# Merged last products, a kept key tile, last queries turned with their keys, and a plain product at the end: one change to an attention and two-MLP kernel

## The chip, the cores and the metric

The kernel runs on one core of a Trainium2 chip. The metric is the device time of one execution in microseconds (us); the median of three runs is compared.

## The reference

```python
# q, k, v: 4 batches x 8 heads x 576 positions x 64, fp32
scores = scale * q @ k.T                       # within a head
mask = (rel >= 0) & (rel < 128)                # a window of 128 keys, causal
scores = where(mask, scores - slope[h] * abs(rel), -1e9)
attn = softmax(scores)                         # sum + 1e-9 in the denominator
x = (attn @ v)  -> [2304 tokens, 512]
x = relu(x @ w_in) ** 2 @ w_out                # 512 -> 2048 -> 512
out = (sigmoid(x @ w_gate) * (x @ w_val)) @ w_out2   # 512 -> 1536 -> 512
```

The weights arrive as 64-bit words and are turned to fp32 in the kernel. Every product of the two MLPs is made of three products of halves (high x high, high x low, low x high).

## The kernel before, in words

**Attention.** The 576 queries of a batch are cut into kinds: "a" (queries 0 to 255), "b" (256 to 511) and "c" (the last 64). A unit is a pair of heads (HP = 4 pairs) of one kind of one batch; a "c" unit takes all four pairs at once. `turn` loads queries and keys of two pairs, transposes them on TensorE (tile `tq` for queries, `tk` for keys; for "c" both go to `tq`, with 64 and 96 rows) and copies them on ScalarE to `qs` and `ks` (`ka` for kind "a", which the "b" units of the same batch read again as their first 128 keys). `attend` then makes the scores (`ts`, lines 638 and 653), masks and adds the slopes on VectorE, takes exp on ScalarE, normalizes, transposes the probabilities (`tp`, line 741), copies them to `pt`, masks them with POOL's selection (line 751), multiplies by the values (`tv`, line 778) and splits the result into a high and a low half of `x` (one ScalarE copy, one VectorE subtraction). An fp32 product is two instructions on TensorE, and the two heads of a pair use different halves of the array's rows or columns, so their instructions stand in pairs.

**First MLP.** The tokens are cut into eight chunks: batch 0 a, batch 0 b, batch 1 a, batch 1 b, then four of 320 tokens that take a "c" part too. For each chunk, 16 steps of `h_step` (tile `h`, lines 804 to 806) and `y_step` (tile `y`, line 841). `h_step` evicts with relu, squares, and splits into `gs`. Attention of later chunks stands between the steps of earlier ones.

**Second MLP.** One block of 256 tokens (`gv`, `o_step`) and four of 512, which use Strassen's seven products: `gv_strassen` for the gate and value products (tiles `pa`, `pd`, line 962), whose result `cg` is split into `ah` with sums `ss`, and `o_strassen` for the output (tiles `o` P1 to P7, line 1120). `sums` loads the summed weights (`so`, `st`) from a scratch in memory. After the last step come two more parts of the last block for pair f = F2 - 4 (one of them) and f = F2 - 2 (both), and then the additions in `oc` and the stores.

**Order.** Nothing is executed in source order. Each operation is registered with `op(...)`: the engines it may run on with a price in ns, what it reads and writes, and a priority (`prio`, a due time in steps). `Plan.schedule` is a list scheduler: it advances a clock, starts on each engine the ready operation of least priority value, and hands out buffers from pools of slots (`CAP` and `CAP0` cap how many a kind may hold; `CAP0` is for chunks 0 to 2). Its order is the order of instructions on each engine. While nothing else is ready in the first 21 us it puts in warm-up products (`warm`). Prices that the change touches: a turn 4 x `pe_ns(128)` = 223 ns, "a" scores 12 x `pe_ns(256)` = 1309 ns, "b" scores 16 x `pe_ns(256)` = 1745 ns.

Of the kernel before, what the change touches and what calls it, by code (L numbers as in the profile page):

```python
# [287 lines left out]
def attention_moe_moe2_kernel(ctx: ExitStack, tc, q, k, v, w_in, w_out1, w_gate, w_val, w_out2, out):  # L288
    nc = tc.nc
# [26 lines left out]
    CAP = {"raw": 3, "nq": 1, "nk": 1, "qs": 2, "ks": 2, "ka": 2, "wt": 6, "vs": 3, "st": 4, "pt": 2, "t": 3,  # L316
           "h": 2, "y": 4, "pg": 2, "pv": 2, "o": 6, "pa": 1, "pd": 1, "pa2": 1, "pd2": 1, "xacc": 2, "ob": 2, "ysg": 2, "raw2": 2, "pp": 2, "xp": 2,
           "tg": 2, "tw": 2, "st2": 5, "so": 5, "xf": 6, "cg": 4, "ss": 2, "ah": 12, "oc": 4, "qc": 3}
    CAP0 = {"nq": 3, "nk": 3, "qs": 2, "ks": 2, "ka": 3, "vs": 5, "st": 5, "pt": 6, "t": 6}
# [220 lines left out]
    X, TURNED, VT = {}, {}, {}  # L540
    FINE = 0

    def values(b, kind, chunk, prio):
# [7 lines left out]
        for h0, h1 in ((0, H // 2), (H // 2, H)) if chunk < FINE else ((0, H),):  # L551
            for t, vn in tiles.items():
                m = min(128, S - 128 * t)
                op({"SP": 250 + 60 * (h1 - h0)}, lambda e, vn=vn, t=t, m=m, h0=h0, h1=h1: nc.sync.dma_start(
                    out=vn()[0:m, h0:h1], in_=v[b, h0:h1, 128 * t:128 * t + m, :].rearrange("h p d -> p h d")),
                   w=[(vn, "v", h) for h in range(h0, h1)], prio=prio, data=182 / 2 * (h1 - h0) * m / 128)

    def turn(b, kind, g, chunk, p):

        early = chunk < 3  # L560
        nq, vq, vk = (2, 128, 128) if kind != "c" else (1, S - 512, (S - 384) // 2)
        a_q, a_k = {"a": (0, 0), "b": (256, 256), "c": (512, 384)}[kind]

        turns = ((0, 1), (1, 2)) if chunk < FINE else ((0, 2),)
        loaded = []
        for src, a, nt, r, name in ((q, a_q, nq, vq, "nq"), (k, a_k, 2, vk, "nk")):
            loaded.append((new(name, [128, nt, 4, 64], F32, early), src, a, nt, r))
        for i0, i1 in turns:
            for t, src, a, nt, r in loaded:
                op({"SP": 250 + 250 * (i1 - i0)}, lambda e, t=t, src=src, a=a, nt=nt, r=r, i0=i0, i1=i1: nc.sync.dma_start(  # L570
                    out=t()[0:r, :, 2 * i0:2 * i1], in_=src[b, 4 * g + 2 * i0:4 * g + 2 * i1, a:a + r * nt, :].rearrange("h (p j) d -> p j h d", j=nt)),
                   w=[(t, i) for i in range(i0, i1)], prio=p(0) - 3, data=2.85 * nt * r * (i1 - i0))

        qs = new("qs", [128, 2, nq * vq], F32, early)
        ks = new("ka" if kind == "a" else "ks", [128, 2, 2 * vk], F32, early)
        banks = [new("tq", [128, 512], F32, early)] * 2 if kind == "c" else [new(kd, [128, 512], F32, early) for kd in ("tq", "tk")]
        parts = ((qs, nq, vq, 0), (ks, 2, vk, 2 * vq if kind == "c" else 0))

        def flip(e, which, i0, i1):
            for z in which:  # L580
                _, nt, v_, c0 = parts[z]
                for i in range(i0, i1):
                    for j in range(nt):
                        nc.tensor.transpose(banks[z]()[:, c0 + (i * nt + j) * v_:c0 + (i * nt + j + 1) * v_],  # L584
                                            loaded[z][0]()[0:v_, j, 2 * i:2 * i + 2].rearrange("p h d -> p (h d)"), C["ident"][0:v_, 0:v_])

        c0 = parts[1][3]
        for i0, i1 in turns:
            for which in ((0, 1),) if kind == "c" else ((0,), (1,)):
                op({"PE": sum(parts[z][1] * 2 * (i1 - i0) * pe_ns(parts[z][2]) for z in which)}, lambda e, which=which, i0=i0, i1=i1: flip(e, which, i0, i1),  # L590
                   cols=.5, r=[(loaded[z][0], i) for z in which for i in range(i0, i1)], w=[(banks[z], z, i) for z in which for i in range(i0, i1)],
                   prio=p(1 + which[0] / 2), also=[parts[z][0] for z in which])
            for i in range(i0, i1):
                op({"ACT": act_ns(nq * vq, True) + 94}, lambda e, i=i: nc.scalar.activation(
                    out=qs()[:, i].rearrange("c (p j) -> c j p", j=nq),
                    in_=banks[0]()[:, i * nq * vq:(i + 1) * nq * vq].rearrange("c (j p) -> c j p", j=nq), func=AF.Copy,
                    scale=C["qmul"][:, 2 * g + i:2 * g + i + 1]), r=[(banks[0], 0, i)], w=[(qs, i)], prio=p(1.3))
            op({"ACT": act_ns(2 * vk * (i1 - i0), True)}, lambda e, i0=i0, i1=i1: nc.scalar.activation(
                out=ks()[:, i0:i1].rearrange("c i (p j) -> c i j p", j=2),
                in_=banks[1]()[:, c0 + 2 * vk * i0:c0 + 2 * vk * i1].rearrange("c (i j p) -> c i j p", i=i1 - i0, j=2), func=AF.Copy),  # L600
               r=[(banks[1], 1, i) for i in range(i0, i1)], w=[(ks, i) for i in range(i0, i1)], prio=p(1.8))
        TURNED[b, kind, g] = qs, ks

    def attend(u, due, long):
# [14 lines left out]
        vkeys = [(t_, "v", h) for t_ in vt.values() for hp in u.hps for h in (2 * hp, 2 * hp + 1)] + [(t_, "pad") for t_ in vt.values()]  # L619
# [4 lines left out]
        def plain(pr):  # L624
# [4 lines left out]
            kprev = TURNED[u.b, "a", groups[0]][1] if kind == "b" else None  # L629

            def go(e):
                if kind == "c":

                    for g, (qs, ks) in enumerate(turned):
                        for x in range(2):
                            for i in range(2):
                                rows = slice(64 * i, 64 * i + 64)
                                nc.tensor.matmul(both[g]()[rows, 256 * x:256 * x + S - 384], qs()[rows, x], ks()[rows, x], start=True, stop=True)
                    return
                qs, ks = turned[0]  # L640
                x = u.hps[0] % 2
                for j in range(nq):

                    if j > 0:
                        todo = [(ks, 0, 0, 256)]
                    elif kind == "b":
                        todo = [(kprev, 128, 0, 128), (ks, 0, 128, 128)]
                    else:
                        todo = [(ks, 0, 0, 128)]
                    for src, k0, c, w_ in todo:  # L650
                        for i in range(2):
                            rows = slice(64 * i, 64 * i + 64)
                            nc.tensor.matmul(both[i]()[:, 256 * j + c:256 * j + c + w_], qs()[rows, x, j * 128:(j + 1) * 128],  # L653
                                             src()[rows, x, k0:k0 + w_], start=True, stop=True)

            mine = sorted({hp % 2 for hp in u.hps})
            rd = [(k_, i) for t_ in turned for k_ in t_ for i in mine] + ([(kprev, i) for i in mine] if kind == "b" else [])
            op({"PE": {"a": 12 * pe_ns(256), "b": 16 * pe_ns(256), "c": 16 * pe_ns(S - 384) + 100}[kind]}, go, r=rd, w=both, prio=pr, also=[st, sm], cols=.5)
# [58 lines left out]
        N = 256  # L717
        cols = 64 if kind == "c" else 128
        if kind == "c":
            xpart = lambda z: x()[:, z, :, n0:n0 + 64]  # L720
        else:
            xpart = lambda z: x()[:, z, u.hps[0], n0:n0 + 256]
        xout = lambda z: [(x, z, hp, u.part) for hp in u.hps]
# [32 lines left out]
        for j in range(nq):  # L756
            if u.q0 + j > 0:
                sel(j, "prev")
            sel(j, "own")
        vp = new("tv", [128, 512], F32, early)  # L760


        prods = []
        if kind != "c":
            h0 = 2 * u.hps[0]
            prods.append((u.q0, h0, lambda i: mid()[:, i].rearrange("p j c -> p (j c)"), 0, 256, True, False))
            if u.q0 > 0:
                prods.append((u.q0 - 1, h0, lambda i: ends()[:, i, 0], 0, 128, False, False))
            prods.append((u.q0 + 1, h0, lambda i: ends()[:, i, 1], 128, 256, False, True))
        else:  # L770
            for hp in u.hps:
                prods.append((3, 2 * hp, lambda i, hp=hp: ends()[:, 2 * hp + i, 0], 64 * hp, 64 * hp + 64, True, False))
                prods.append((4, 2 * hp, lambda i, hp=hp: mid()[:, 2 * hp + i, 0], 64 * hp, 64 * hp + 64, False, True))

# [5 lines left out]

        op({"PE": sum(4 * pe_ns(pr_[4] - pr_[3]) + 46 for pr_ in prods) + 54}, go, cols=.5, r=vkeys + ks_,
           w=[vp], prio=p(9), also=[x])
        if kind == "c":
            vpart = lambda: vp()[:, :N].rearrange("p (c t) -> p c t", t=64)
        else:
            vpart = lambda: vp()[:, :N]
# [145 lines left out]
    def sums(n, kind, f, prio):  # L932
        after = [W["out2", F2 - 4, 22], ("scr", ("out2", F2 - 2), 7)] if n == 1 and f == 0 else []
        TW[n, kind, f] = dict(zip(("P6", "P7", "P5", "P4"),
# [9 lines left out]
    def gv_strassen(n, kind, f, e0):  # L944
# [86 lines left out]

        p3 = new("ah", [128, 512], F32R)
# [75 lines left out]
    def o_strassen(n, f, part, e0, last=False):  # L1108


        t0, NB = blocks[n]
        ops, wts = A2[n, f], TW[n, "out2", f]
# [12 lines left out]
        for i in range(6 * part, 6 * part + 6):  # L1125
            name, t = OO[i // 2], i % 2
            o = O[n][name]
            op({"PE": 3 * pe_ns(256)}, lambda e, name=name, t=t, o=o: go(name, t, o, f == 0, f == F2 - 2),
# [153 lines left out]
```

## Time and profile before

| | us |
|---|---|
| median of 3 runs | 970.33 (968.18 to 972.26) |
| the profiled execution, whole | 969.7 |
| its span, first to last instruction | 967.9 |
| TensorE busy in the span | 950.9 (98%) |
| VectorE, ScalarE, POOL busy | 622.3, 566.3, 192.0 |

The prediction is read against the profiled execution; the 1.8 us around its span belong to the time too. A matmul's duration overlaps the next one, so the distance between starts is the price of one.

### The profile page before, as it was taken

The page shows a single profiled execution, that of the slowest core. Times are in us where ns is not written, and L with a number is a line of the kernel's source. Part 1 is how long each engine was busy: PE and PEld are TensorE (multiplying, and loading weights), DVE is VectorE, ACT ScalarE, POOL GpSimd, SP SyncE. Part 2 cuts the span into 40 slices and gives each one's busy share as a digit, 9 for nine tenths or more (in the row PEclk, how much of TensorE's full clock was granted, in tenths as well). Part 3 has the DMA queues.
Part 4 walks back from the last instruction along what each step waited for, and adds up shares of the span by engine and source line. Part 5 has one row for each costly group of instructions (what it writes and reads, how often), then busy time and mean ns, then how long its engine had stood idle before and what let it go on. Part 6 is the DMA issues. An engine that isn't in the chain of part 4 may idle for free.

```text
span 967.9 us, 21379 instructions
## 1 busy us (share of the span) xinstructions
PE 950.9 (98%) x7728; PEld 913.6 (94%) x7728; DVE 622.3 (64%) x1608; ACT 566.3 (59%) x1496; POOL 192.0 (20%) x277
## 2 busy tenths in 40 slices
PE   8899999999999999999999999999999999999997
PEld 6589999989999998999999999999999999999997
DVE  7999986777676687677552133645765585476555
ACT  6988777668677677576654422544544544454442
POOL 3611112223224112112200000102211230222001
PEclk9989999999999999999999999999999999999999
DMA  9765446584664873963599941566776687678931
GB/s 229 174 178 163 151 121 206 175 264 160 193 206 158 230 213 133 264 209 136 158 348 376 385 143 34 189 215 225 252 254 210 214 279 223 212 241 264 348 113 45
DMA packets 181929, 200.64 MB, mean 207 GB/s; under 512 B 80192, under 2 KB 113472, under 8 KB 181824
## 3 DMA queue, kind: packets, MB, share of 16 engines
q1 hardware_dynamic: 181824, 199.27, 65.1%
q8 instruction: 62, 1.02, 0.4%
q14 instruction: 43, 0.35, 0.1%
HBM read 152.04 MB, written 47.19 MB: 206 GB/s over the span
## 4 chain that ended last, share of the span: by engine, by line
PE 91%; ACT 3%; DMA 2%; DVE 2%; POOL 1%; SPq 1%; issue 0%; POOLq 0%; DVEq 0%; ACTq 0%
PE y L841 21%; PE pa L962 14%; PE pd L962 11%; PE o L1120 10%; PE h L804 7%; PE h L805 7%; PE h L806 7%; PE tv L778 3%; PE ts L653 2%; PE o L1087 2%; PE pd L1120 2%; PE tp L741 1%; PE tq L584 1%; ACT st L685 1%; DMA nq<-in_q_dram 1%; DMA wscr<-pp 1%
## 5 line engine op out<-in xcount | busy, mean ns | idle before, releaser
L841 PE MATMUL y<-gs,wh 128*128 128x256 f32 (+1 forms) x1024 | 216.0, 303 | 3.7 <-DVE gs L335 2.8
L841 PEld LDWEIGHTS y<-gs,wh 128*128 128x128 f32 x1024 | 165.1, 191 | 10.3 <-issue 4.8
L804 PE MATMUL h<-x,wh 128*128 128x256 f32 (+1 forms) x512 | 155.0, 303 | 0.6 <-ACT pt L745 0.6
L841 PE MATMUL y<-gs,wl 128*128 128x256 f32 (+1 forms) x512 | 152.2, 297 | 0.0
L805 PE MATMUL h<-x,wh 128*128 128x256 f32 (+1 forms) x512 | 151.2, 295 | 0.0
L806 PE MATMUL h<-x,wl 128*128 128x256 f32 (+1 forms) x512 | 151.1, 295 | 0.0
L338 ACT ACTIVATE cg<-pa 128x256 f32<-128x256 f32 x144 | 54.8, 382 | 109.4 <-PE pa L962 105.9
L335 DVE TENSOR_TENSOR gs<-r,gs 128x320 fp32r<-128x320 f32 (+1 forms) x115 | 54.7, 475 | 72.1 <-ACT gs L338 71.6
L804 PEld LDWEIGHTS h<-x,wh 128*128 128x128 f32 x512 | 96.7, 189 | 4.2 <-issue 1.9
L841 PEld LDWEIGHTS y<-gs,wl 128*128 128x128 f32 x512 | 97.7, 191 | 0.0
L818 ACT ACTIVATE r<-h 128x256 f32<-128x256 f32 (+1 forms) x128 | 51.9, 406 | 76.8 <-PE h L806 76.3
L805 PEld LDWEIGHTS h<-x,wh 128*128 128x128 f32 x512 | 96.7, 189 | 0.0
L806 PEld LDWEIGHTS h<-x,wl 128*128 128x128 f32 x512 | 96.6, 189 | 0.0
L962 PE MATMUL pa<-x,st 128*128 128x256 f32 x576 | 84.2, 282 | 0.0
L751 POOL TENSOR_SCALAR_AFFINE_SELECT pt<-pt 128x256 f32<-128x256 f32 (+1 forms) x120 | 62.8, 549 | 106.5 <-ACT pt L745 105.5
L978 DVE TENSOR_TENSOR cg<-cg,pd 128x256 f32<-128x256 f32 x96 | 40.4, 421 | 61.0 <-PE pd L962 59.7
L962 PEld LDWEIGHTS pa<-x,st 128*128 128x128 f32 x576 | 75.1, 189 | 0.0
L1120 PE MATMUL o<-wr,ah 128*128 128x256 f32 x432 | 70.4, 281 | 0.2 <-DVE ah L335 0.2
L1120 PE MATMUL o<-so,ah 128*128 128x256 f32 x432 | 66.3, 281 | 0.0
L685 ACT ACTIVATE st<-st,sm 128x128 f32<-128x128 f32 x144 | 56.4, 397 | 10.7 <-DVE sm L678 10.7
L338 ACT ACTIVATE gs<-r 128x256 fp32r<-128x256 f32 (+1 forms) x128 | 56.6, 442 | 9.1 <-PE y L841 2.6
L1120 PEld LDWEIGHTS o<-wr,ah 128*128 128x128 f32 x432 | 59.5, 189 | 0.4 <-DVE ah L335 0.4
(179 smaller groups left out, 2050.4 us busy)
## 6 DMA issues: line engine op xcount, KB each, us to landing
st<-wscr SPq DMA_DIRECT2D x192, 256.0 KB, 3.4
wscr<-pp SPq DMA_DIRECT2D x72, 512.0 KB, 3.4
so<-wscr SPq DMA_DIRECT2D x96, 256.0 KB, 3.5
raw<-in_moe_w_out_dram SPq DMA_DIRECT2D x28, 512.0 KB, 3.8
wr<-wscr SPq DMA_DIRECT2D x54, 256.0 KB, 5.4
raw<-in_moe_w_in_dram SPq DMA_DIRECT2D x16, 512.0 KB, 4.7
vs<-in_v_dram SPq DMA_DIRECT2D x24, 256.0 KB, 5.1
raw<-in_moe_w_gate_dram SPq DMA_DIRECT2D x12, 512.0 KB, 4.3
```

Of the source, the lines that this page charges most:

```text
L335: return lambda e: eng(e).tensor_tensor(out=out(), in0=a(), in1=b(), op=ALU.subtract)
L338: return lambda e: nc.scalar.activation(out=out(), in_=in_(), func=AF.Copy, scale=scale)
L685: op({"ACT": 386}, lambda e, x=x: nc.scalar.activation(out=st()[:, x, :], in_=st()[:, x, :], func=AF.Exp, bias=sm()[:, x:x + 1], scale=-1. ...
L751: op({"POOL": pool_sel(512 // nq)}, lambda e: nc.gpsimd.affine_select(out=pt_of(what, j), in_=pt_of("own", j), pattern=[[0, 512 // (nq * c ...
L804: nc.tensor.matmul(ps()[:, :N], w[0]()[:, c], x()[:, 0, cc, :N], start=cc == 0, stop=False)
L805: nc.tensor.matmul(ps()[:, :N], w[0]()[:, c], x()[:, 1, cc, :N], start=False, stop=False)
L806: nc.tensor.matmul(ps()[:, :N], w[1]()[:, c], x()[:, 0, cc, :N], start=False, stop=cc == CC - 1)
L818: op({"ACT": act_ns(N, True)}, lambda e: nc.scalar.activation(out=g()[:, :N], in_=ps()[:, :N], func=AF.Relu), r=[ps], w=[g], prio=ep, also ...
L841: nc.tensor.matmul(y()[:, c0:c0 + N], w[a]()[:, c], gs()[:, b, :N], start=f == 0 and p == 0 and n != 1, stop=f == F1 - 1 and p == 2, skip_ ...
L962: nc.tensor.matmul(ps()[:, :256], w()[:, z * 256 + cc * 128:z * 256 + cc * 128 + 128], x, start=start and cc == 0 and i == 0, stop=cc == 1 ...
L978: op({"DVE": dve_ns(256)} if psum else dve_or_pool(256), lambda e: eng(e).tensor_tensor(out=quarter(i, j)(), in0=quarter(i, j)(), in1=src( ...
L1120: nc.tensor.matmul(o()[:, 256 * t:256 * t + 256], a_()[:, c_ + 128 * t:c_ + 128 * t + 128], w()[:, 256 * z:256 * z + 256], start=start and ...
```

## The change

There are four edits and new prices for the scheduler. (1) From chunk 3 on, the last product of an even unit ("a" or "b") is put off until the odd unit of its two pairs is ready; both go into one bank `tv` in one operation, and one copy and one subtraction of 512 columns move them to `x`. (2) The "b" turn writes its keys into two tiles of 384 columns, one for each pair; a copy on ScalarE or POOL puts the last 128 keys of the "a" tile ahead of them. The "b" scores then read one tile: two products of 256 columns for each head instead of one of 256 and two of 128. (3) For "c", one tile holds the 64 last queries and the 64 last keys, another the 128 keys before; four transposes of 128 rows a turn replace six, and both tiles are loaded once for a batch. (4) For the last pair of the last block, the seven Strassen products are replaced by eight plain ones; the sums of the earlier pairs' products are taken in `oc` before it, the results added as they come, and the last one stored in two halves. Prices: a turn 436, scores of "a" and "b" 1056, of "c" 1643 ns. `pt` may hold 4 slots instead of 2, `ks` 3 instead of 2.

```diff
-    CAP = {..."ks": 2, ... "pt": 2, ...}
+    CAP = {..."ks": 3, ... "pt": 4, ...}
-    CAP0 = {... "ks": 2, ...}
+    CAP0 = {... "ks": 4, ...}
...
+    MERGE = 3
...
     def turn(b, kind, g, chunk, p):
...
+            qs = new("qs", [128, 2, 256], F32, early)
+            ks = [new("ka", [128, 2, 256], F32, early)] if kind == "a" else [new("ks", [128, 384], F32, early) for _ in range(2)]
...
+                op({"PE": 436}, flip, cols=.5, r=[loaded[z]], w=[bank], prio=p(1 + z / 2), also=[qs] if z == 0 else ks)
...
+                else:
+                    for i in range(2):
+                        op({"ACT": act_ns(256, True)}, lambda e, i=i, bank=bank: nc.scalar.activation(
+                            out=ks[i]()[:, 128:384].rearrange("c (p j) -> c j p", j=2),
+                            in_=bank()[:, 256 * i:256 * i + 256].rearrange("c (j p) -> c j p", j=2), func=AF.Copy), r=[bank], w=[(ks[i], 1)], prio=p(1.8))
...
+                def carry(e, i=i):
+                    if e == "ACT":
+                        nc.scalar.activation(out=ks[i]()[:, 0:128], in_=before[i]()[:, 128:256], func=AF.Copy)
+                    else:
+                        nc.gpsimd.tensor_copy(ks[i]()[:, 0:128], before[i]()[:, 128:256])
...
+        if g == 0:
+            own, prev = LAST[b] = new("nq", [128, H, 64], F32, early), new("nk", [128, H, 64], F32, early)
+            for t, src, r0, a0, n in ((own, q, 0, 512, S - 512), (own, k, S - 512, 512, S - 512), (prev, k, 0, 384, 128)):
...
+        def flip(e):
+            for z, t in enumerate((own, prev)):
+                for i in range(2):
+                    nc.tensor.transpose(bank()[:, 256 * z + 128 * i:256 * z + 128 * i + 128],
+                                        t()[:, 4 * g + 2 * i:4 * g + 2 * i + 2].rearrange("p h d -> p (h d)"), C["ident"])
...
+                    k0, w_ = (128 * j, 256) if kind == "b" else (0, 128 + 128 * j)
+                    for i in range(2):
+                        rows = slice(64 * i, 64 * i + 64)
+                        nc.tensor.matmul(both[i]()[:, 256 * j:256 * j + w_], qs()[rows, x, j * 128:(j + 1) * 128],
+                                         ks[x]()[rows, k0:k0 + w_], start=True, stop=True)
...
-            op({"PE": {"a": 12 * pe_ns(256), "b": 16 * pe_ns(256), "c": 16 * pe_ns(S - 384) + 100}[kind]}, go, r=rd, w=both, prio=pr, also=[st, sm], cols=.5)
+            op({"PE": {"a": 1056, "b": 1056, "c": 1643}[kind]}, go, r=rd, w=both, prio=pr, also=[st, sm], cols=.5)
...
+        PROBS[u.b, kind, u.hps[0]] = mid, ends
+        both = kind != "c" and u.chunk >= MERGE
+        if both and u.hps[0] % 2 == 0:
+            return
         vp = new("tv", [128, 512], F32, early)
...
+        hps = [u.hps[0] - 1, u.hps[0]] if both else u.hps
...
     def sums(n, kind, f, prio):
+        if (n, kind, f) == (nblk - 1, "out2", F2 - 2):
+            TW[n, kind, f] = {ij: W[kind, f, ij] for ij in (11, 21, 22)}
+            TW[n, kind, f][12] = fetch("so", (kind, f), PIECE[kind][12], prio, after)
+            return
...
+        if (n, f) == (nblk - 1, F2 - 2):
+            A2[n, f] = {}
+            for i in (1, 0):
+                hi, lo = new("ah", [128, 512], F32R), new("ah", [128, 512], F32R)
+                for j in range(2):
+                    cs = slice(256 * j, 256 * j + 256)
+                    op({"ACT": act_ns(256)}, copy(lambda hi=hi, cs=cs: hi()[:, cs], quarter(i, j)), r=[(c[i], j)], w=[(hi, j)], prio=pr, also=[lo])
+                    op({"DVE": dve_ns(256)}, minus(lambda lo=lo, cs=cs: lo()[:, cs], quarter(i, j), lambda hi=hi, cs=cs: hi()[:, cs]),
...
+        if n == nblk - 1 and f == F2 - 4 and part == 1:
+            u, u3, v, w = OC[n] = [new("oc", [128, 512], F32) for _ in range(4)]
+            op({"ACT": act_ns(512, True)}, copy(u, o["P1"]), r=[o["P1"]], w=[u], prio=pr)
+            add(u3, u, o["P6"])
+            add(v, u3, o["P7"])
+            add(u3, u3, o["P5"])
+            add(w, v, o["P5"])
...
+    def o_last(n, f, part, e0):
+        if part == 0:
+            todo = [(1, 0, PAD["pd"], v, True), (1, 1, PAD["pa"], w, True)]
+        else:
+            todo = [(0, 0, o["P2"], u, False), (0, 1, o["P3"], u3, False)]
+        for z, (i, j, ps, sum_, fresh) in enumerate(todo):
+            fine = (i, j) == (0, 1)
+            for t in range(2):
+                for part_ in range(2):
+                    (hi, ch, kh), (lo, cl, kl) = ops[i, part_]
+                    wt = wts[10 * part_ + 11 + j]
...
+                    op({"PE": 3 * pe_ns(256)}, go, r=[(hi, kh), (lo, kl), wt, ps], w=[ps if not fine else (ps, t)],
+                       prio=e0 + z + .2 * t + .1 * part_)
...
```

## Rows read from the trace of the kernel before

**Rows 1.** The page: its head and the busy table's first line.

```profile
span 967.9 us, 21379 instructions
...
PE 950.9 (98%) x7728; PEld 913.6 (94%) x7728; DVE 622.3 (64%) x1608; ACT 566.3 (59%) x1496; POOL 192.0 (20%) x277
```

**Rows 2.** Stretches: us, PE, PEld, DVE, ACT, POOL busy (count), clock, DMA, GB/s.

```profile
20.00:30.00 10.00, 9.60 (x90) 6.25 (x87) 8.81 (x48) 10.00 (x40) 6.28 (x10) 1.00 0.95 234
...
45.00:50.00 5.00, 2.16 (x17) 1.79 (x14) 4.82 (x18) 5.00 (x21) 1.96 (x4) 0.79 0.52 99
50.00:55.00 5.00, 5.00 (x27) 4.78 (x28) 4.77 (x13) 2.70 (x6) 0.00 (x0) 0.53 0.70 200
...
300.00:500.00 200.00, 200.00 (x1526) 186.57 (x1525) 135.89 (x388) 134.58 (x366) 40.68 (x66) 1.00 0.65 203
```

**Rows 3.** Timeline of TensorE near 48 us: start, duration, instruction, idle before.

```profile
48.67 0.58 PE L841 MATMUL y<-gs,wh 128*128 128x256 f32 x1 [2.84 <-DVE gs L335]
```

**Rows 4.** Timeline of TensorE: one burst of an "a" unit's last products.

```profile
145.90 0.28 PE L806 MATMUL h<-x,wl 128*128 128x256 f32 x1
146.11 0.87 PE L778 MATMUL tv<-pt,vs 128*64 128x256 f32 x8
146.91 0.38 PE L841 MATMUL y<-gs,wh 128*128 128x256 f32 x1
```

**Rows 5.** The same, two "a" units that stand together.

```profile
143.75 1.52 PE L778 MATMUL tv<-pt,vs 128*64 128x256 f32 x16
145.20 0.39 PE L804 MATMUL h<-x,wh 128*128 128x256 f32 x1
```

**Rows 6.** Timeline of TensorE: a "c" turn, and an "a" turn's queries.

```profile
312.62 0.31 PE L806 MATMUL h<-x,wl 128*128 128x320 f32 x1
312.86 0.33 PE L584 MATMUL tq<-identr,nq 64*128 64x64 f32 x2
313.13 0.55 PE L584 MATMUL tq<-identr,nk 96*128 96x96 f32 x4
313.46 0.54 PE L841 MATMUL y<-gs,wh 128*128 128x320 f32 x2
...
339.88 0.31 PE L806 MATMUL h<-x,wl 128*128 128x320 f32 x1
340.03 0.60 PE L584 MATMUL tq<-identr,nq 128*128 128x128 f32 x4
340.39 0.54 PE L841 MATMUL y<-gs,wh 128*128 128x320 f32 x2
```

**Rows 7.** Timeline of TensorE: the scores of a "b" unit.

```profile
419.22 0.49 PE L653 MATMUL ts<-ka,qs 64*128 64x128 f32 x4
419.55 0.82 PE L653 MATMUL ts<-ks,qs 64*128 64x128 f32 x8
420.30 0.56 PE L841 MATMUL y<-gs,wh 128*128 128x320 f32 x2
```

**Rows 8.** Groups by line and form: count, busy us, mean ns, idle before.

```profile
L598 ACT ACTIVATE ks<-tk 128x512 f32<-128x512 f32 x8 | 5.2, 646 | 1.6 <-PE tk L584 1.6
```

**Rows 9.** Timeline of POOL in the first microseconds: a copy.

```profile
3.11 0.28 POOL L397 COPY relc<-rel 64x128 f32<-64x128 f32 x1
```

**Rows 10.** Timeline of the last 12 us, all engines.

```profile
955.75 0.42 DVE L335 TENSOR_TENSOR ah<-cg,ah 128x256 fp32r<-128x256 f32 x1
955.84 1.10 PE L1120 MATMUL o<-wr,ah 128*128 128x256 f32 x8
...
957.16 1.45 PE L1120 MATMUL o<-wr,ah 128*128 128x256 f32 x10 [0.23 <-DVE ah L335]
...
960.28 3.46 DVE L1145 TENSOR_TENSOR oc<-o,oc 128x512 f32<-128x512 f32 x5
...
961.27 0.87 PE L1120 MATMUL o<-wr,ah 128*128 128x256 f32 x6
...
963.28 1.26 POOL L1169 TENSOR_TENSOR oc<-oc,xacc 128x512 f32<-128x512 f32 x1 [4.68 <-DVE oc L1145]
```

More of the change, by code (lines that the diff above doesn't have):

```diff
@@ L550, in values @@
                 op({"POOL": 150 + 2.1 * 512}, lambda e, vn=vn, m=m: nc.gpsimd.memset(vn()[m:128], 0.0), w=[(vn, "pad")], prio=prio)
-        for h0, h1 in ((0, H // 2), (H // 2, H)) if chunk < FINE else ((0, H),):
+        for h0, h1 in ((0, H),):
             for t, vn in tiles.items():
@@ L556, in values @@
                    w=[(vn, "v", h) for h in range(h0, h1)], prio=prio, data=182 / 2 * (h1 - h0) * m / 128)
+    LAST = {}
     def turn(b, kind, g, chunk, p):
         early = chunk < 3
[L561 to L601, printed above, removed]
@@ new lines, in turn @@
+        m = S - 512
+        qs, ks, bank = new("qs", [128, 2, m], F32, early), new("ks", [128, 2, 128 + m], F32, early), new("tq", [128, 512], F32, early)
+        def flip(e):
+            for z, t in enumerate((own, prev)):
+                for i in range(2):
+                    nc.tensor.transpose(bank()[:, 256 * z + 128 * i:256 * z + 128 * i + 128],
+                                        t()[:, 4 * g + 2 * i:4 * g + 2 * i + 2].rearrange("p h d -> p (h d)"), C["ident"])
+        op({"PE": 436}, flip, cols=.5, r=[(own, 0), (own, m), (prev, 0)], w=[bank], prio=p(1), also=[qs, ks])
@@ new lines, in turn @@
+        for i in range(2):
+            op({"ACT": act_ns(m, True) + 94}, lambda e, i=i: nc.scalar.activation(
+                out=qs()[:, i], in_=bank()[:, 128 * i:128 * i + m], func=AF.Copy, scale=C["qmul"][:, 2 * g + i:2 * g + i + 1]),
+               r=[bank], w=[(qs, i)], prio=p(1.3))
+        for z, (c0, c1) in enumerate(((128, 128 + m), (0, 128))):
+            op({"ACT": act_ns(2 * (c1 - c0), True)}, lambda e, z=z, c0=c0, c1=c1: nc.scalar.activation(
+                out=ks()[:, :, c0:c1], in_=bank().rearrange("c (z i p) -> c z i p", z=2, i=2)[:, z, :, (128 - m if z == 0 else 0):], func=AF.Copy),
+               r=[bank], w=[(ks, z)], prio=p(1.8))
@@ L604, in attend @@
+        TURNED[b, kind, g] = qs, [(lambda i=i: ks()[:, i]) for i in range(2)], [[(ks, 0), (ks, 1)]] * 2
     def attend(u, due, long):
@@ L628, in plain @@
             turned = [TURNED[u.b, kind, g] for g in groups]
-            kprev = TURNED[u.b, "a", groups[0]][1] if kind == "b" else None
             def go(e):
                 if kind == "c":
-                    for g, (qs, ks) in enumerate(turned):
+                    for g, (qs, ks, _) in enumerate(turned):
                         for x in range(2):
@@ L716, in attend @@
         n0 = 256 * u.part
-        N = 256
         cols = 64 if kind == "c" else 128
[L719 to L723, printed above, removed]
         shape = [128, 2, 2, 128] if kind != "c" else [128, 2 * HP, 1, 64]
@@ L1111, in o_strassen @@
         t0, NB = blocks[n]
+        if (n, f) == (nblk - 1, F2 - 2):
+            return o_last(n, f, part, e0)
+        stop_at = F2 - 4 if n == nblk - 1 else F2 - 2
         ops, wts = A2[n, f], TW[n, "out2", f]
@@ L1172, in attention_moe_moe2_kernel, with go @@
     OC = {}
+    def o_last(n, f, part, e0):
+        t0, NB = blocks[n]
+        ops, wts, o = A2[n, f], TW[n, "out2", f], O[n]
+        u, u3, v, w = OC[n]
+        if part == 0:
[8 more added lines that the diff above has]
+                    wt = wts[10 * part_ + 11 + j]
+                    def go(e, t=t, part_=part_, hi=hi, lo=lo, ch=ch, wt=wt, ps=ps, fresh=fresh):
+                        for k, (a_, y) in enumerate(((hi, 0), (hi, 1), (lo, 0))):
+                            nc.tensor.matmul(ps()[:, 256 * t:256 * t + 256], a_()[:, ch + 128 * t:ch + 128 * t + 128], wt()[:, 256 * y:256 * y + 256],
+                                             start=fresh and t == 0 and part_ == 0 and k == 0, stop=part_ == 1 and k == 2, skip_group_check=True)
+                    op({"PE": 3 * pe_ns(256)}, go, r=[(hi, kh), (lo, kl), wt, ps], w=[ps if not fine else (ps, t)],
+                       prio=e0 + z + .2 * t + .1 * part_)
+                if fine or t == 1:
+                    cs = slice(256 * t, 256 * t + 256) if fine else slice(0, 512)
+                    key = (ps, t) if fine else ps
+                    op({"DVE": dve_ns(256 if fine else 512)}, lambda e, ps=ps, sum_=sum_, cs=cs: nc.vector.tensor_tensor(
+                        out=sum_()[:, cs], in0=ps()[:, cs], in1=sum_()[:, cs], op=ALU.add), r=[key, sum_], w=[(sum_, t) if fine else sum_], prio=e0 - 2)
+                    r0, m = t0 + 256 * i + (128 * t if fine else 0), 128 if fine else 256
+                    op({"SP": 475}, lambda e, sum_=sum_, cs=cs, r0=r0, m=m, j=j: nc.sync.dma_start(
+                        out=out[r0:r0 + m, 256 * j:256 * j + 256].rearrange("(t p) c -> p t c", p=128),
+                        in_=sum_()[:, cs].rearrange("p (t c) -> p t c", c=256)), r=[(sum_, t) if fine else sum_], prio=e0, data=728)
     WA = [("in", 0)]
```

100 lines of the change are left out of this document (66 added, 34 removed).

## The prediction

> **What bounds the kernel now.** I read four things, from the whole to the single instruction.
>
> First the page's busy table: TensorE is busy 98% of a span of 967.9 us [rows 1]. A busy share alone doesn't show a bound, so second the table of stretches. From 300 to 500 us TensorE is busy all 200 us at full clock, while VectorE and ScalarE are busy 136 and 135 of 200 [rows 2]. There a copy more or less on those two costs nothing, and a TensorE slot saved is time saved. The start is different: from 20 to 30 us ScalarE is busy 10.0 of 10 us and VectorE 8.8; from 45 to 50 us TensorE works only 2.2 us and its granted clock is 0.79, then 0.53 up to 55 us, which means mostly the lower of its two levels, 1.2 instead of 2.4 GHz [rows 2]. Third, the timeline there names the cause: a y product at 48.67 us waited 2.84 us for VectorE's gs [rows 3]. Fourth, since TensorE is the bound, I need the price of each small group of products. The "busy" of a pipelined matmul overlaps its neighbour (0.28 us long, but 0.12 us after the last one), so I take prices from start to start in the timeline.
>
> **Merged last products (chunks 3 to 7: 20 units in 10 pairs).** The columns are the same; what goes is one of two bursts. A lone burst of a kind "a" unit starts 0.21 us after the last h product, where 0.12 is the spacing, and the y product follows 0.80 us later: 1.01 in all, so the burst costs 1.01 - 0.12 = 0.89 [rows 4]. Two such units that happened to stand together, 16 instructions, took 1.45 from their first to the next h product [rows 5]: the second eight add 1.45 - 0.80 = 0.65. A merge saves 0.89 - 0.65 = 0.24. Where the burst already stands behind scores, its entry (0.21 - 0.12 = 0.09) is saved anyway, so 0.15. Ten pairs: 1.5 to 2.4; I take 2.1, nearer the upper end, as most bursts stand alone. The even unit waits for the odd one; its copies to x come later, but the last unit of a chunk comes when it did, with one 512-wide copy and one subtraction in place of two each. ScalarE and VectorE have a third of their time free there [rows 2].
>
> **Last queries turned with their keys (8 turns).** Six transposes (two with 64 rows, four with 96) become four with 128. Before: 312.62 to 313.46 is 0.84, less one h slot of 0.15 (a slot of 320 columns: 339.88 to 340.03): 0.69. Four full transposes: 339.88 to 340.39 is 0.51, less 0.15: 0.36 [rows 6]. Saving 0.33 a turn, 2.7 in all; as bounds 2.4 (a slot or two at the old entry price) and 2.8. The four loads per batch become three, on SP, which isn't late there; the one copy of keys becomes two on ScalarE, covered as above.
>
> The Trainium skill speaks for and against here. "TensorEngine Tiling (Array Packing)", Key Properties, says that a change of tiling mode drains TensorE, which agrees with the 0.21 and 0.24 us entries [rows 4, 6]. "TensorE: Matmul & The Clock Gate", Back-to-back issue gap, prices a product by its columns, N/2.4 + 2.5 ns: by that, six transposes (my estimate 228 ns) and four (223 ns) cost the same and the saving is nothing. The measured 0.69 against 0.36 decides; the rule is kept as a rival.
>
> **Kept key tile (16 "b" units).** Scores were six pairs of passes, four 128 and two 256 wide; now four 256 wide. Of the 1.08 us, the two 128 pairs from the "a" tile take 0.33 and the rest, two of 128 and two of 256, 0.75 [rows 7]. With 0.09 for leaving (as for entering, rows 4) and a 256 pair twice a 128 pair, 6c = 0.66, c = 0.11: so the first two carry 0.11 over their columns. After: 8c + 0.09 = 0.97, saving 0.11. If a 256-wide first pair pays the same 0.11, nothing is saved. A 256 pair already lasts 0.22, longer than that first pair did, so I take 0.11. Only 12 of the units lie in the stretch that TensorE bounds; the four of batch 0 lie at 20 to 35 us. So 0 to 1.3, taken 1.3. The price is on the other engines: each of 8 turns evacuates keys in two ScalarE copies where one took 0.65 [rows 8], and adds two copies of 128 columns on POOL or ScalarE; the nearest row is POOL's copy of 64x128 in 0.28 [rows 9]. From 60 us on that is covered [rows 2]. In the first 45 us ScalarE has no cover: two turns, each some 0.2 us of fixed cost, and four carries of about 0.3: from nothing (they land on POOL between selections) to 1.6 us. I take 0.3.
>
> **Eight products at the end.** Seven Strassen products of 6 instructions (42) become eight of 6 (48): 6 x 0.12 = 0.7 more. Removed: four combinations and the halves that hang on them. TensorE's wait there, 0.23 us in the row and 0.4 with the lost slots [rows 10], ends with it, because the first of the new operands are plain quarters, split as soon as the gating multiply ends. So TensorE ends at about 962.14 + 0.7 - 0.4 = 962.4. Behind it, before: VectorE's row of five additions of 0.69 ends at 963.74, then POOL adds from 963.28 to 964.54, and store and closing take 967.9 - 964.54 = 3.4 [rows 1, 10]. After: half an addition, 0.42 (a 256-wide VectorE pass [rows 10]), then the same 3.4 or a little less for half the bytes: 962.4 + 0.1 + 0.4 + 3.4 = 966.3, a gain of 1.6. What can be late is VectorE: from 955.05 it has four splits of 0.42, the addition to xacc, three to four of the sums taken in advance and five final ones: 1.7 + 0.7 + 2.8 + 2.9 = 8.1 us, to about 963.1 where 962.9 is needed. So 0.7 to 2.1, taken 1.4. Three loads of weights fewer are hidden.
>
> **The start.** Everything is placed by a list scheduler whose prices change: a turn 223 to 436 ns, "a" scores 1309 to 1056, "b" scores 1745 to 1056. So the order of the first 60 us can change although the work hardly does. What lies there to win or lose is the wait of 2.8 us and the slow stretch behind it: from 48.67 to 55 us, some 6 us, at about half the clock, so some 3 us more than at the higher level [rows 2, 3]. Bounds: 6 us gained, 6 lost; I take none, and the 0.3 above.
>
> **Sum.** 2.1 + 2.7 + 1.3 + 1.4 - 0.3 = 7.2 us. The profiled execution took 969.7 us (span 967.9, 1.8 around it): 962.5. The median of the three runs shown is 0.6 above that execution, so 963.1; call it 963.0. A measurement of this kernel tells about 0.5%, 4.9 us, from no change: below 965.5 is faster, above 975.2 slower.
>
> **Rivals.**
> - *The start reorders against us.* The gs wait gets longer or the scores of batch 0 wait for carried keys, and 2.5 to 5 us are lost: 965.5 to 968. For it: ScalarE has no free time from 20 to 30 us. Against it: the added work is 1.6 us at most. Chance 0.17, a quarter of it still below 965.5.
> - *The start reorders for us.* gs comes early enough, the clock doesn't fall at 48 us, 3 to 6 us are gained: 957 to 960. Chance 0.12.
> - *TensorE goes by columns.* All three edits of the attention keep their columns (512 for a "c" turn, 512 per "b" scores, merged products likewise). If the entries are paid anyway, in other places, only the tail is left: 969.7 - 1.4 = 968.3, with the median's 0.6 about 968.9. Against it are rows 4 to 6, where neighbours are the same and the bursts differ. Chance 0.07. (The skill's rule on the issue gap says this.)
> - *Slower: a second slow stretch.* The same y wait at the start, on VectorE's gs, lasts so long that chunk 1's products also run at 1.2 GHz. One stretch like the present one costs 2.8 + 3 = about 6 us [rows 2, 3]; the gain of 7.2 is gone when that y product starts later than about 56 us instead of 48.67. One and a half such stretches more give 972, two give 975. Against it: loads and first turns don't change. Chance 0.05, half of it above 975.2.
>
> The forecast itself, 960.5 to 965.5, has 0.59.
>
> **Numbers.** Below 965.5: 0.59 + 0.12 + 0.04 = 0.75. Above 975.2: 0.02, rounded to 0.03. Between: 0.22. Range: from 958.5, which leaves half of the good start out (0.06), to 967.8, which leaves out the rivals by columns and slower and little else (0.13).
>
> **What would show it.** Right: "c" turns with four transposes and 0.36 between neighbours; ten bursts of 16 or 24 tv instructions at 0.65 to 0.85 for the second unit; "b" scores of eight instructions in about 0.97; the y product of rows 3 near 48 us; TensorE ending with its last product, one half addition and one store behind it, 3.9 us to the end. Wrong: a TensorE wait in the middle for x or a bank held by an unmerged pair, that y product several us later, or VectorE ending far behind TensorE in the tail.

## The result and the profile after

The changed kernel takes 958.49 us (median of 3 runs, 957.54 to 959.99) against 970.33: a ratio of 0.9882 [0.9856, 0.9908], so it is faster by 11.8 us where 7.3 were forecast. That is the very edge of the range ("from 958.5"), outside the forecast itself (960.5 to 965.5), and the time of the rival in which the start reorders for us. The profiled execution took 957.54, its span 955.4.

The page, as [rows 1]:

```profile
span 955.4 us, 21188 instructions
...
PE 941.8 (99%) x7656; PEld 908.9 (95%) x7656; DVE 630.4 (66%) x1621; ACT 559.8 (59%) x1496; POOL 186.4 (20%) x270
```

The stretches, as [rows 2]:

```profile
20.00:30.00 10.00, 9.13 (x78) 6.33 (x78) 8.99 (x57) 10.00 (x44) 5.54 (x13) 1.00 1.05 235
45.00:50.00 5.00, 3.90 (x34) 2.76 (x32) 4.82 (x18) 3.73 (x14) 0.01 (x1) 1.00 0.12 44
50.00:55.00 5.00, 3.94 (x33) 3.06 (x34) 4.90 (x26) 3.91 (x16) 1.93 (x2) 1.00 0.65 171
300.00:500.00 200.00, 200.00 (x1515) 189.62 (x1515) 136.79 (x378) 129.17 (x353) 38.09 (x60) 1.00 0.67 204
```

In the middle nothing has changed its kind: TensorE works all 200 us, the other engines have a third of their time free. At the start it has: from 45 to 55 us the granted clock stays at 1.00, the level of 2.4 GHz, where it was 0.79 and 0.53. The y product that waited 2.84 us at 48.67 [rows 3] starts at 41.27 after 1.28. TensorE's timeline, its waits between 41 and 55 us:

```profile
41.27 0.39 PE L870 MATMUL y<-gs,wh 128*128 128x256 f32 x1 [1.28 <-DVE gs L335]
...
50.57 0.92 PE L679 MATMUL ts<-ka,qs 64*128 64x128 f32 x6 [1.36 <-DVE x L335]
...
54.84 0.39 PE L834 MATMUL h<-x,wh 128*128 128x256 f32 x1 [0.49 <-DVE x L335]
```

**Small groups of products.** From the same timeline, a "c" turn, "b" scores, and merged last products of "a" and of "b" units, each with its neighbours:

```profile
303.48 0.31 PE L835 MATMUL h<-x,wl 128*128 128x320 f32 x1
303.63 0.38 PE L624 MATMUL tq<-identr,nq 128*128 128x128 f32 x2
...
304.42 0.54 PE L870 MATMUL y<-gs,wh 128*128 128x320 f32 x2
...
356.06 0.31 PE L870 MATMUL y<-gs,wl 128*128 128x320 f32 x1
356.30 1.52 PE L806 MATMUL tv<-pt,vs 128*64 128x256 f32 x16
357.75 0.41 PE L833 MATMUL h<-x,wh 128*128 128x320 f32 x1
...
408.92 1.13 PE L679 MATMUL ts<-ks,qs 64*128 64x256 f32 x8
409.98 0.41 PE L833 MATMUL h<-x,wh 128*128 128x320 f32 x1
...
430.98 0.31 PE L870 MATMUL y<-gs,wl 128*128 128x320 f32 x1
431.21 1.96 PE L806 MATMUL tv<-pt,vs 128*64 128x256 f32 x24
433.10 0.56 PE L870 MATMUL y<-gs,wh 128*128 128x320 f32 x2
```

Both "c" turns of a batch stand together: 304.42 - 303.48 less a slot of 0.15 is 0.79, so 0.40 a turn against 0.69 [rows 6]. Two merged "a" units cost 357.75 - 356.06 - 0.15 = 1.54, against twice 0.89 [rows 4]: 0.24 saved, as the two of [rows 5]. The "b" scores are what was misjudged: 408.92 to 409.98 is 1.06, against 1.08 [rows 7]. They save 0.02, not 0.11. The starts of the single products in the two traces show why: before, the first two instructions of 128 columns (one for each head) stand 0.21 us ahead of the next two, and those only 0.11 ahead of the ones behind them; after, the first two of 256 columns stand 0.32 ahead, the next two 0.22. The first step costs 0.10 more at either width.

**The copies.** Groups by line and form:

```profile
L338 ACT ACTIVATE x<-tv 128x512 fp32r<-128x512 f32 x10 | 5.9, 591 | 3.9 <-PE tv L806 3.8
L594 ACT ACTIVATE ks<-tk 128x256 f32<-128x256 f32 x16 | 5.7, 402 | 1.7 <-PE tk L580 1.7
L604 ACT ACTIVATE ks<-ka 128x128 f32<-128x128 f32 x13 | 3.7, 300 | 0.0
```

Ten merges, as counted. The keys of a turn take 2 x 402 ns where one copy took 646 [rows 8], so 0.16 more, and 13 of the 16 carries (the copies of the "a" tile's last keys) went to ScalarE at 0.30 each, near POOL's 0.28 [rows 9]; the three on POOL took 0.46.

**The end**, as [rows 10]: VectorE and TensorE in the timeline of the last 12 us.

The multiply before, and then the end of the changed kernel:

```profile
954.35 0.69 DVE L1007 TENSOR_TENSOR cg<-cg 128x512 f32<-128x512 f32 x1
```

```profile
943.47 0.69 DVE L1040 TENSOR_TENSOR cg<-cg 128x512 f32<-128x512 f32 x1
...
945.53 0.60 PE L1254 MATMUL pd<-wr,ah 128*128 128x256 f32 x3
...
948.44 1.58 PE L1254 MATMUL o<-wr,ah 128*128 128x256 f32 x12
...
951.12 0.42 DVE L1262 TENSOR_TENSOR oc<-o,oc 128x256 f32<-128x256 f32 x1 [0.37 <-PE o L1254]
...
951.60 0.62 PE L1254 MATMUL o<-wr,ah 128*128 128x256 f32 x3 [0.52 <-DVE oc L1262]
952.25 0.43 DVE L1262 TENSOR_TENSOR oc<-o,oc 128x256 f32<-128x256 f32 x1 [0.71 <-PE o L1254]
```

From the gating multiply (943.47; 954.35 before) TensorE needs 8.75 us to its end at 952.22, where it needed 7.79. Behind it come one half addition and a store: 3.2 us to the end of the span, where there were 5.8. There is a wait that nobody forecast: the last three products wait 0.52 us for VectorE to read the first half of the bank `o`, though they write the other half.

**Where the time went.** I cut each trace at two marks: the start of the product that follows the first 600 of the first MLP (`h` and `y`), and the first product of the second MLP. The first two stretches are called the start and the middle below.

| us | to product 600 | to the second MLP | to the end | span |
|---|---|---|---|---|
| before | 132.1 (130.9) | 416.8 (418.0) | 419.0 | 967.9 |
| after | 125.9 | 411.8 | 417.7 | 955.4 |
| gained at equal work | 5.0 | 6.2 | 1.4 | 12.5 |
| forecast | -0.3 | 6.1 | 1.4 | 7.2 |

Before had one "b" unit's scores more behind it at the first mark, 1.32 less a slot of 0.15 = 1.17 us; in brackets the times with that moved over. The last two columns came as forecast. All that was missed lies in the first 130 us.

### The profile page after: what moved, and what is told of

Its sections match the earlier page's. It is cut to its first block, busy times and chain, and to the rows that moved or that the text cites. A ratio compares the mean times of both kernels' runs of the same rounds, so it can differ in the third digit from the quotient of the medians.

```text
span 955.4 us, 21188 instructions
## 1 busy us (share of the span) xinstructions
PE 941.8 (99%) x7656; PEld 908.9 (95%) x7656; DVE 630.4 (66%) x1621; ACT 559.8 (59%) x1496; POOL 186.4 (20%) x270
## 4 chain that ended last, share of the span: by engine, by line
PE 94%; DVE 3%; ACT 1%; DMA 1%; SPq 1%; issue 0%; DVEq 0%
PE y L870 22%; PE pa L995 14%; PE pd L995 11%; PE o L1168 10%; PE h L833 7%; PE h L834 7%; PE h L835 7%; PE tv L806 3%; PE ts L679 2%; PE o L1132 2%; PE pd L1168 2%; PE tp L761 1%; DMA nq<-in_q_dram 1%; ACT st L711 1%; PE ts L670 1%; PE pv L1104 1%
## 5 line engine op out<-in xcount | busy, mean ns | idle before, releaser
L335 DVE TENSOR_TENSOR gs<-r,gs 128x256 fp32r<-128x256 f32 (+1 forms) x122 | 58.0, 476 | 64.7 <-ACT gs L338 64.4
L1168 PE MATMUL o<-wr,ah 128*128 128x256 f32 x414 | 68.0, 281 | 0.0
L1168 PE MATMUL o<-so,ah 128*128 128x256 f32 x414 | 64.0, 281 | 0.0
L1168 PEld LDWEIGHTS o<-wr,ah 128*128 128x128 f32 x414 | 57.3, 189 | 0.0
```

The lines of the kernel that those rows point to most:

```text
L335: return lambda e: eng(e).tensor_tensor(out=out(), in0=a(), in1=b(), op=ALU.subtract)
L1168: nc.tensor.matmul(o()[:, 256 * t:256 * t + 256], a_()[:, c_ + 128 * t:c_ + 128 * t + 128], w()[:, 256 * z:256 * z + 256], start=start and ...
```

## The experiments

Two theories stood at the outset: that the start was won by the new prices alone, through the order; or that the edits of the attention are worth more than they were priced. Times are medians, and the marks come from one profiled execution of each kernel; the kernel before took 970.27, 969.59 and 970.34 beside the three groups of runs.

**1. The new prices alone, in the kernel before.**

```diff
-op({"PE": sum(parts[z][1] * 2 * (i1 - i0) * pe_ns(parts[z][2]) for z in which)}, lambda ...
+op({"PE": 436}, lambda ...
-op({"PE": {"a": 12 * pe_ns(256), "b": 16 * pe_ns(256), "c": 16 * pe_ns(S - 384) + 100}[kind]}, go, ...
+op({"PE": {"a": 1056, "b": 1056, "c": 1643}[kind]}, go, ...
```

> The kernel before, with nothing but the scheduler's new prices (a turn 436 ns, scores of a and b 1056, of c 1643). Theory A, the new prices alone put the start in a better order: the slow stretch at 45 to 55 us is gone, the 600th product of the first MLP starts 3 to 5 us earlier than the 132.1 us of before, and the time is 965 to 967.5 us. Rival B, the start was won by the work itself (keys in tiles of their own): 969 to 971 us, the start as before. Rival C, any disturbance moves the start at random: a start that moves by several us, either way, with no change in price for one unit of work.

966.39 us, 0.9954 [0.994, 0.9968]: 3.9 faster with not one product changed. The five executions (965.57 to 967.41) all lie below the nine of the kernel before (969.31 to 971.87), and the mean granted clock is the same in both, 0.994 to 0.997. To the three marks: 127.65, 417.9, 419.0, so 3.3 us won in the start and nothing behind it. Its own start isn't smooth. TensorE's timeline, and the stretch from 40 to 50 us:

```profile
40.81 1.65 PE L653 MATMUL ts<-ka,qs 64*128 64x128 f32 x8 [3.33 <-ACT ka L598]
```

```profile
40.00:50.00 10.00, 9.19 (x58) 7.21 (x58) 9.79 (x30) 7.32 (x21) 3.61 (x7) 0.66 0.38 111
```

A wait of 3.33 us and a granted clock of 0.66 behind it: the stall of [rows 3] was not avoided, it came 8 us earlier, on another wait, and the products behind it came earlier too, by 4 to 5 us for products 40 to 300 of `h` and `y`.

**2. The changed kernel with the old prices.**

```diff
-op({"PE": 436}, flip, ...
+op({"PE": 8 * pe_ns(128) / 2}, flip, ...          # "c": 2 * pe_ns(64) + 4 * pe_ns(96)
-op({"PE": {"a": 1056, "b": 1056, "c": 1643}[kind]}, go, ...
+op({"PE": {"a": 12 * pe_ns(256), "b": 16 * pe_ns(256), "c": 16 * pe_ns(S - 384) + 100}[kind]}, go, ...
```

> The changed kernel with the old prices of the scheduler (turn 223 ns, c turn 228, scores 1309, 1745, 1419), all four edits kept. Theory A: the start loses 3 to 5 us again, 961.5 to 964 us, with a wait of about 3 us and a lower clock near 45 to 55 us. Rival B: 958 to 959.5 us, the start as in the changed kernel. Rival C: anything between 956 and 965, by the start alone, while the stretch from the 600th product to the end stays within 0.5 us of the changed kernel's.

964.03 us, 0.993 [0.9918, 0.9943]: 5.5 slower than the changed kernel, and near the 963.0 that was forecast without a gain at the start. Marks: 132.5 (132.9 with a turn of 0.36 that it had not yet done), 411.9, 417.8. The stretches from 40 to 60 us, and TensorE's waits there:

```profile
40.00:50.00 10.00, 8.17 (x70) 6.21 (x70) 9.82 (x27) 8.63 (x27) 4.07 (x9) 1.00 0.51 157
50.00:60.00 10.00, 5.35 (x45) 3.96 (x46) 9.90 (x34) 7.10 (x23) 1.29 (x1) 0.99 0.58 163
```

```profile
51.08 0.92 PE L679 MATMUL ts<-ka,qs 64*128 64x128 f32 x6 [2.32 <-DVE x L335]
55.15 1.09 PE L806 MATMUL tv<-pt,vs 128*64 128x256 f32 x12 [1.55 <-DVE x L335]
...
59.72 0.57 PE L834 MATMUL h<-x,wh 128*128 128x256 f32 x1 [1.38 <-DVE x L335]
```

Up to 60 us the clock is full, and the start is late all the same: VectorE is busy 9.9 of 10 us, and TensorE waits for it at three places. The clock falls only behind these waits (0.84 from 60 to 70 us). The larger pools of `pt` and `ks` are in this kernel too, so they did not win the start.

What VectorE does instead can be read. At each of the three places its subtraction for `x` could start when ScalarE's copy ends; the third of them, with the copy:

```profile
57.32 0.37 ACT L338 ACTIVATE x<-tv 128x256 fp32r<-128x256 f32 x1
57.61 1.72 DVE L432 SCALAR_TENSOR_TENSOR wt<-raw,wt 128x512 int32<-128x512 int32 x1
59.26 0.41 DVE L335 TENSOR_TENSOR x<-tv,x 128x256 fp32r<-128x256 f32 x1
```

The copy ends at 57.69 and the subtraction starts 1.6 us later, behind a conversion of weights (`wt`) that takes 1.72 us where others of its line take 0.69; at the other two places it is 0.9 and 1.1. In the changed kernel there are two such places (50.10 and 54.37), of 0.8 and 0.6. No run moved these conversions alone.

**3. No merged last products.**

```diff
-    MERGE = 3
+    MERGE = 99
```

> The changed kernel without merged last products (each unit has its own bank and burst again). By the price of a burst: 1.5 to 2.4 us slower, 960 to 961 us, all of it after the third chunk begins, with the start and the end as they are. By the rival that TensorE goes by columns: 958 to 959 us.

961.21 us, 0.9903 [0.9889, 0.9917]. Marks: 126.9, 415.0, 417.2. The middle is 3.2 us longer (2.1 forecast). Ten bursts at 0.24 give 2.4 of it; the rest came with the order, in the neighbours of other bursts and in plain slots. The second MLP is 0.5 shorter, so 2.7 in all are left.

**4. The seven products at the end.**

```diff
...
-        if (n, f) == (nblk - 1, F2 - 2):
-            return o_last(n, f, part, e0)
-        stop_at = F2 - 4 if n == nblk - 1 else F2 - 2
+        stop_at = F2 - 2
...
-        if n == nblk - 1 and f == F2 - 4 and part == 1:
+        if False:
```

> The changed kernel with Strassen's seven products for the last pair of the last block again. Forecast: 1.4 us slower (0.7 to 2.1), 959.5 to 960.5 us: TensorE ends about 1 us earlier relative to the last value product, but 6 us instead of 3.5 lie behind its last product. Rival, the end is given by the last store and its closing alone, whatever stands ahead of it: no difference beyond 0.3 us.

961.46 us, 0.9905 [0.9891, 0.9918]. The last column is 419.5; the three runs with seven products give 419.0, 419.0 and 419.5, the first eight with the new end 417.2 to 417.9. Against the changed kernel's two profiles (417.7, 417.9) the end is worth 1.1 to 1.8, as forecast. But the start was later too, 128.6, although its instructions stand in the same order as the changed kernel's on every engine for the first 910 us. That is taken up at the end.

**5. The changed kernel again, as a control.**

> The changed kernel once more, as a control for the others of this call: 957.5 to 960 us. If the granted clock at 40 to 60 us differs from the first profile's 1.00, the start can move by up to 2.6 us between two executions of the same order; otherwise the 600th product of the first MLP starts at 125.9 us within 0.5.

958.9 us, 0.9893 [0.9875, 0.9911]. Marks: 126.7, 411.8, 417.9. The start differs by 0.8, the middle by nothing in the second decimal (411.78 both).

**6. "b" units that read the "a" tile again.**

```diff
-ks = ... [new("ks", [128, 384], F32, early) for _ in range(2)]      # and the carries
+ks = ... [new("ks", [128, 2, 256], F32, early)]
...
+elif kind == "b":
+    todo = [(kprev[1], 128, 0, 128), (ks, 0, 128, 128)]
```

The pools of `ks` are set back to 2 with it, as before the change.

> The changed kernel without the kept key tile: b units read their first 128 keys from the a tile again, no copies, scores in twelve instructions; new prices kept. By the price of the scores: 1.3 us slower behind the start (0 to 1.9), so 959.5 to 960.5 us if the start stays. Rival B of the first call, the start was won by the tiles: 963 us, a start later by 4 us. If a first product of 256 columns paid the same entry as one of 128, nothing: 958.5 us.

959.41 us, 0.9898 [0.9882, 0.9914], not told apart from the control. Marks: 126.8, 413.0, 417.7. The middle is 1.2 longer, about what was forecast, but not for the forecast's reason: the ten units in it spend 0.15 more inside their scores. At two places alone, 134.80 and 167.48, slots of 0.12 last 0.36 and 0.49, 0.6 together; they are slots of `y` products, not of the scores, and come with the order without carries. Up to 164 us that order is the one of experiment 1 on every engine, with a start of 126.8 here and 127.7 there: two kernels without the kept key tile, and neither has lost the early start. So the tile did not win it.

**7. The old last turn.**

```diff
-for t, src, r0, a0, n in ((own, q, 0, 512, S - 512), (own, k, S - 512, 512, S - 512), (prev, k, 0, 384, 128)):
+for src, a, nt, r, name in ((q, 512, nq, vq, "nq"), (k, 384, 2, vk, "nk")):      # loads and six transposes for each turn
```

> The changed kernel with the last queries and keys turned as before (six transposes with 64 and 96 rows a turn, loads for each turn), at the new price 436. By the bursts: 2.7 us slower (2.4 to 2.8), 960.9 to 961.5 us, all of it behind 240 us. By columns alone: nothing, 958.5 us.

961.88 us, 0.9917 [0.9903, 0.9931]. Marks: 128.3, 414.2, 417.5. The middle is 2.4 us longer, 0.30 for each of eight turns (0.33 forecast). The later start again comes with an order that is the same for the first 210 us.

**8 and 9. Other prices: those of the trace, and some 10% up.**

```diff
-436 for a turn; scores 1056, 1056, 1643
+357; 945, 1055, 1540                    # 8: as the trace has them
+480; 1160, 1160, 1800                   # 9
```

> The changed kernel with the scheduler's prices set to what the trace shows for a burst between two products (turn 357, a scores 945, b 1055, c 1540). Theory A1, the start is better the nearer the prices are to the trace: as fast as the changed kernel or up to 2 us faster, 956.5 to 959 us. Theory A2, any other order is a throw: the start moves by 1 to 5 us either way, and the rest by less than 0.5 us; then 957 to 964 us.

> The changed kernel with the scheduler's prices a tenth above the changed ones (turn 480, scores 1160, c scores 1800). A1, nearer to the trace is better: 0.5 to 2 us slower than the changed kernel. A2, any other order is a throw: the 600th product anywhere from 125 to 132 us, the rest within 0.5 us of the changed kernel's 829.5, the whole 957 to 964 us.

959.46, 0.9897 [0.9881, 0.9914], and 960.99, 0.9909 [0.9895, 0.9924]. Starts at equal work: 129.0 (128.3 and two turns of 0.36) and 129.3 (128.2 and one unit's scores); middles 411.3 and 411.6. So prices nearer to the trace gave no better start, and a tenth more didn't either; experiment 8 can't be told from the changed kernel by its time. Both starts are still earlier than either with the old prices.

**10 and 11. The last half in a bank of its own; and that with two more merges.**

```diff
+                c0 = 256 * t
+                if fine and t == 1:
+                    ps, fresh, c0 = o["P1"], True, 0
...
-    MERGE = 3
+    MERGE = 2          # 11 only
```

> The changed kernel with the second half of the last product in a bank of its own (the bank of P1, free by then; the half of P3 gathered before is added to the sum early). Theory: the wait of TensorE for VectorE's addition of the first half, 0.5 us in the row and 0.7 between starts, comes from both halves lying in one bank; it goes, TensorE's last product and all behind it come 0.6 us earlier, the time from the first product of the last pair to the end shrinks by 0.5 to 0.7 us. Rival, it waits for something else (the sum tile or the order): no change. In the whole time 0.6 us is hardly to be told: 957.5 to 959 us.

> The same and merging from the third chunk on (batch 1, a), two merges more. By the price of a burst 0.25 us for each merge: 0.5 us less in the stretch behind the 600th product, 957 to 958.5 us, if the order of the start does not change by it; by the theory that any other order is a throw, the start moves by up to 3 us either way.

958.29, 0.9887 [0.9871, 0.9902], and 958.27, 0.9875 [0.9858, 0.9891]. The wait is gone; timeline of the tenth kernel:

```profile
952.29 0.51 PE L1258 MATMUL o<-wr,ah 128*128 128x256 f32 x3
...
952.84 0.42 DVE L1266 TENSOR_TENSOR oc<-o,oc 128x256 f32<-128x256 f32 x1 [0.29 <-PE o L1258]
```

From the first product of the last pair (946.88 here, 945.53 after) to this addition it is 5.96 us against 6.72, so 0.76 won; but to the end of the span 9.73 against 9.87. Experiment 11, with the same end, takes 5.97 and 9.28 (from 947.73): there 0.59 of it is kept, as forecast. What experiment 10 loses lies behind its last store: from the store's landing to the end of the span it has 1.41 us, the changed kernel and experiment 11 have 0.97; why, was not settled. The two more merges take 0.2 off the middle (411.6), not the 0.5 expected, and the start of experiment 11 is later, 128.4, in an order that is the changed kernel's up to 138 us. Neither version can be told from the changed kernel by its time.

## Why the prediction was right and wrong

**What bounds it: right.** The middle and the second MLP gained 7.6 us where 7.5 were forecast, in a stretch in which TensorE hardly stands still (no wait at all in the middle). What was taken from TensorE there came off the end.

**Merges: right in kind, small by a third.** 2.4 by the bursts, as priced at 0.24; 3.2 in the middle and 2.7 to the end by experiment 3, against 2.1.

**"c" turns: right.** 2.4 against 2.7. A turn costs 0.40, not the 0.36 of an "a" turn.

**Kept key tile: the price was wrong.** The step was "the first two carry 0.11 over their columns", inferred from two sums. The new scores take 1.06 where 0.97 was forecast: a 256-wide first pair pays nearly the same, 0.10. That is the lower bound that the text named. Twelve units at 0.02 are 0.2, not 1.3. What experiment 6 loses beyond that came from the order; 6.2 - 3.2 - 2.4 leaves 0.6 for both together. That the middle as a whole came out (6.2 against 6.1) is luck in part: the key tile gave some 0.7 to 1.1 less than it was priced, the merges with the order around them 0.6 to 1.1 more.

**The end: right in sum, wrong in its parts.** 1.4 for the whole of the second MLP, 1.6 from the gating multiply on; but TensorE took 1.0 longer, not 0.3, since the half bank's wait came in; behind it 2.6 were saved, not 1.9. VectorE was not late.

**The start: the step that failed.** "Bounds: 6 us gained, 6 lost; I take none, and the 0.3 above." It gained 5.0 in the profile and 4.2 in the control. The result lies on the very edge of the range (958.49 against 958.5), and the range reaches that far only because half of this rival was let in: that is luck. Experiments 1 and 2 show what did it: the prices, 3.9 us put in alone, 5.5 taken out alone, in the profiles nearly all of it in front of product 600. The rival that came true named the place and the size, but its mechanism (gs early enough, so the clock doesn't fall) is only half of it: the changed kernel did keep its clock, and yet experiment 1 won 3.3 us of start with the clock down, and experiment 2 had a late start with the clock up. What is left is the order in which VectorE (after, busy 9.8 of 10 us from 40 to 60) and ScalarE (10 of 10 from 20 to 40) serve TensorE. In experiment 2 the subtractions for `x` are seen to stand behind conversions of weights; that this is the pair that matters was not tested alone. Four orders made with other than the old prices (the changed kernel's, the one that experiments 1 and 6 share, and those of 8 and 9) have starts of 125.9 to 129.3, the two with the old ones 130.9 and 132.9. Four against two don't show that a new order is better for its prices, and not by chance. Nor is all of the 5.0 the order's: starts of one and the same order lie up to 2.6 us apart, the late ones where the clock fell (last section), and in the profile of before it had fallen too [rows 2]. Rows of before could not give this size; but for prices that change by a factor of 1.2 to 2 a gain deserved more than the chance of 0.12.

**The other rivals.** By columns, the turns and merges would have given nothing. Experiments 3 and 7 lose 3.2 and 2.4 us in the middle, so the groups are not priced by columns. The formula that the prediction took from the Trainium skill ("TensorE: Matmul & The Clock Gate", Back-to-back issue gap) is given there for a single isolated product, with the remark that it under-counts for few columns; no run here tests it on one. The rows show what is missing for groups: entry and exit. Neither a start against us nor a second slow stretch came.

## What to carry to other kernels

Where a list scheduler places everything, a change of its prices is an edit of its own: run it alone first, and give it a chance on both sides where two engines are full. Price small groups of products from start to start with their neighbours, and don't split one sum into two unknowns by assumption: the 0.11 that was put on the narrow pair belonged to a first pair of either width. To account for a result, cut the traces at marks of equal work; here the middle repeated to 0.01 us, and the whole miss showed in one column.

## What the runs showed of the hardware

**Two halves of a bank were not free of each other.** In the changed kernel a product into columns 256 to 511 of a bank waited 0.52 us while VectorE read columns 0 to 255; with a bank of its own the wait was gone (experiment 10). It is a wait on a semaphore; whether the chip would need it was not tried.

**The same order doesn't give the same start.** Seven profiles have the changed kernel's order on every engine up to 138 us or longer: its own two and experiments 3, 4, 7, 10 and 11. In four of them the granted clock is 1.00 in every stretch up to 130 us, and product 600 starts at 125.9, 126.7, 126.9 and 126.8. In the other three, experiments 4, 7 and 11, it falls somewhere, and they reach it at 128.6, 128.3 and 128.4. From 14 to 18 us, in the stretches of the changed kernel, of experiment 4 and of experiment 7:

```profile
14.00:18.00 4.00, 3.71 (x33) 3.14 (x31) 3.91 (x14) 2.84 (x10) 1.51 (x3) 1.00 1.24 257
```

```profile
14.00:18.00 4.00, 3.99 (x25) 3.66 (x27) 3.56 (x12) 2.38 (x8) 0.72 (x1) 0.69 1.14 240
```

```profile
14.00:18.00 4.00, 3.98 (x21) 3.94 (x21) 3.85 (x13) 1.78 (x7) 0.72 (x1) 0.57 1.17 251
```

With granted clocks of 1.00, 0.69 and 0.57 TensorE gets through 33, 25 and 21 products. In experiment 4 the clock falls again, to 0.81 and 0.85 between 50 and 60 us; in experiment 11 it falls only later:

```profile
35.00:40.00 5.00, 5.00 (x33) 4.66 (x32) 4.57 (x19) 3.83 (x16) 3.05 (x5) 0.74 0.83 140
```

The clock goes with the loss; that it is the cause of all of it, and what lets it fall, stays open. It is no matter of the kernel alone: of four executions of experiment 10, three with mean clocks of 0.999 to 1.000 took 958.22 to 958.31, and the one with 0.996 took 961.19. Nor is the clock all: one of experiment 5 took 960.05 at 1.000, where the three others took 958.5 to 958.9. It means that of a change at the start of this kernel some 2 us can't be put down to the order, and that one profile of a start is not enough.
